# Moving one store, one turn of u and some sums between the slots of VectorE's program in a gated attention and MoE kernel

## The chip, the cores and the metric

The kernel runs on one core of a Trainium2 chip. The metric is the device time of one execution in microseconds (us); of several runs the median is taken. All times below are from such runs or from the hardware profile of one of them. Engines are named as in the profile: PE is TensorE, PEld its weight loads, DVE is VectorE, ACT is ScalarE, POOL is GpSimd, SP is SyncE, which here only issues DMAs.

## The reference

There are 8 batches of 3008 rows. For each batch the first half computes a gated attention without softmax, and the second half a feed-forward block on all 24064 rows:

```
scores = z @ z.T / S                 # z: 3008 x 64
attn   = maximum(scores, 0) ** 2
x      = u * (attn @ v)              # u, v: 3008 x 256
h      = x @ w_in                    # 256 -> 2048
g      = h * sigmoid(1.702 * h)
out    = g @ w_out                   # 2048 -> 256
```

## The kernel before

**Stages of a batch.** The rows of a batch are cut into six chunks of 512 columns (numbered 0 to 5; the last has 448). `attend` (L486) walks over a chunk in steps n = 0, 1, 2, ...; each step issues one or two matmuls on PE that add one key block's part to the chunk's accumulator (L529). A full chunk has 47 steps. Between the steps the main loop (L974) puts other work into each engine's queue: blocks of scores (`scores`, L247, squared by `square`, L268 and L282), loads, turns and sums. Since scores are symmetric, squared blocks are turned by DMA on SP (`turn_unit`, L310; L275, L289) and used for other chunks too. When a chunk is done, DVE multiplies its two accumulators with u (`gate`, L546), which gives x in the tile xt and frees the accumulators.

**Chunk 4** of batches 1 to 6 (`split`, L336) is done in another way, by `attend_split` (L426): seven products P1 to P7 instead of eight (Strassen's scheme), in 42 steps of two 256-column matmuls each (L440). The products need sums of score blocks, S1 to S4, and of value blocks, which DVE computes (`score_form`, L380, with lines L392, L394, L396, L383 for S1, S2, S4, S3; `value_forms`, L363). `fills` (L466) lists for each of these sums the slot (chunk, step) in which it goes into DVE's queue. The last of the three pairs of chunks (t = 2) has its eight half sums in chunk 4 itself. Some products share an accumulator: P6, P7 and P4 add to the bank of P1. So after the last step of P7, DVE must have added that bank to the tile ya (L458) before P4 may write to the bank again.

**Heads and tails.** The feed-forward part of a batch has 48 groups q = 0 to 47 (`up_group`, L569). A group is four matmuls to the tile hg (L584), a gelu on ACT to the tile gf (L597, with two buffers for hg and two for gf), and a scaled copy to the tile gt, by DVE (L603) or in some groups of the tail by ACT (L601). Groups 0 to 15 ("heads", LAGY = 16) are issued among the steps of chunk 4, from step 2 on; groups 16 to 47 come after chunk 5, one by one with the products of the output matrix (`pair_product`, L737, matmuls L757). These too are seven products instead of eight for each pair of chunks s = 0, 1, 2, and need block sums S1 to S4 of gt, 16 for each pair (`pair_sum`, L710: L719, L721, L723, L714). They wait in a list, SUMS. `some_sums(most)` (L621) puts the next one into DVE's queue, or the next two if more than `most` wait. In heads of a split batch it is called for q = 8, 9, 10, 12, 13 and 14 (L604), in the tail for each q (L598). A product whose sum is still missing takes it from the list itself (L754).

**Stores and turns.** `store` (L854) turns a chunk's result y into the tile yo on DVE (L859) and issues four or more DMAs on SP (L869). yo has one buffer, so the next store's turn waits until the DMAs of the one before have landed. Tile y has two buffers; the z of the next batch is staged in y buffers too (`stage_z`, L160, on POOL's queue in chunk 4, step 4). The results of the last two chunks of a batch are stored in the next batch: they wait in LAST2, and the main loop takes one at chunk 3, step 4, and one at chunk 3, step 26 (L987). `turn_u` (L210) turns a loaded chunk of u (tile uq, loaded on POOL's queue, L207) into the tile ut on DVE (L214), which `attend_split` first needs for P3 (L460). A small POOL copy, `hold` (L993), at chunk 4, step 4, keeps POOL's queue from loading u until the turned blocks of chunks 4 and 5 have landed.

**What sets the order.** Each engine works its queue in the order in which the program issues. Nothing reorders it. So a slot in these tables is a place in DVE's queue: an instruction that waits there holds all behind it.

```
slots += [(4, n) for n in (12, 12, 14, 14, 16, 18, 20, 22)]                      # L475
if not pair or LAGY > q >= (LAGY // 2 if split(b, NCH - 2) else 0) and q % 4 < 3:  # L604
    some_sums(8)
TURNS = {(1, NJ + 4): 2, (2, NJ + 4): 3, (4, 24): 4, (5, 8): 5}                  # L904
if (i, n) in ((3, 4), (3, 26) if more else (4, 14)) and LAST2:                   # L987
    LAST2.pop(0)()
```

Of the kernel before, what the change touches and what calls it, by code (L numbers as in the profile page):

```python
# [15 lines left out]
def kernel(  # L16
# [20 lines left out]
    NJ = (S + P - 1) // P  # L37
# [3 lines left out]
    NCH = (S + CH - 1) // CH  # L41
# [294 lines left out]
    def split(b, i):  # L336

        return i == NCH - 2 and 0 < b < B - 1
# [127 lines left out]
    def fills(b):  # L466

        VT.clear()
        SA.clear()
        at = {(0, 19): [lambda: pool.tensor_copy(VZ[TOP], V16[b][TOP, NJ - 1])]}  # L470
        slots = [(0, n) for n in (20, 23, 26, 28)] + [(1, n) for n in (27, 31, 35, 39, 43)]
        slots += [(2, n) for n in (19, 21, 23)]
        ops = [op for t in range(3) for op in value_forms(b, t)]
        slots += [(2, n) for n in (28, 33, 38, 43)] + [(3, n) for n in (30, 34, 41, 44)]
        slots += [(4, n) for n in (12, 12, 14, 14, 16, 18, 20, 22)]  # L475
        ops += [op for t in range(3) for op in score_forms(b, t)]
        assert len(ops) == len(slots)
        for where, op in zip(slots, ops):
            at.setdefault(where, []).append(op)
        return at  # L480
# [82 lines left out]
    def paired(b, s):  # L563

        return b < B - 1 or s < NCH // 2 - 1
# [3 lines left out]
    def up_group(b, q):  # L569
        s, r = divmod(q, 2 * NFG)  # L570
        pair = paired(b, s)
        if pair:
            fg, e = (TILES if q >= 2 * NFG or b else TILES0)[r // 2], r % 2
            if fg >= NFG // 2:
                e = 1 - e
            k = 2 * s + e
        else:
            k, fg = divmod(q, NFG)
        i, n = blocks(b)[k]
        hg = ps2.tile([P, FFG, CH], F32, name="hg", tag="ps2")  # L580
        for e in range(FFG):
            ff = fg * FFG + e
            for c in range(NCC):
                pe.matmul(  # L584
                    hg[:, e, :n], W1[:, c, ff * P:(ff + 1) * P], XT[b, i][:, c, :n],
                    start=(c == 0), stop=(c == NCC - 1),
                )
        if pair:
            if r % 2 == 0:
                GT[b, s, fg, "pair"] = pa.tile([P, FFG, 2, CH], F16, name="gt", tag="tt", bufs=14)  # L590
            g = GT[b, s, fg, "pair"][:, :, k % 2, :n]
        else:
            if fg % 2 == 0:
                GT[b, k, fg // 2] = pa.tile([P, CB, CH], F16, name="gt", tag="tt", bufs=14)
            g = GT[b, k, fg // 2][:, (fg % 2) * FFG:(fg % 2 + 1) * FFG, :n]
        gf = pw.tile([P, FFG, CH], F32, name="gf", tag="gf")
        act.activation(gf[:, :, :n], hg[:, :, :n], AF.Gelu_apprx_sigmoid, scale=1.0 / FSC)  # L597
        if pair and q >= LAGY:  # L598
            some_sums(3 if q % 2 else 8)
        if q >= LAGY and q % 8 in (1, 3, 5):  # L600
            act.activation(g, gf[:, :, :n], AF.Copy, scale=FSC)  # L601
        else:
            dve.tensor_scalar(g, gf[:, :, :n], FSC, None, ALU.mult)  # L603
        if not pair or LAGY > q >= (LAGY // 2 if split(b, NCH - 2) else 0) and q % 4 < 3:  # L604
            some_sums(8)
        if pair:
            some = (("S1", "S2", "S3"), ("S4",))[r % 2] if fg >= NFG // 2 else ()
            SUMS.extend([(s, "S1 S2 S4 S3".index(m), lambda m=m: pair_sum(b, s, fg - NFG // 2, m)) for m in some])
            SUMS.sort(key=lambda x: x[:2])
            if r == 2 * NFG - 2 and s == NCH // 2 - 1:  # L610
                some_sums(8)
        elif fg in (NFG - 3, NFG - 1):
            SUMS.extend([(s, 0, x) for x in left_sums(b, k, fg == NFG - 1)])
# [220 lines left out]
    LAST2 = []  # L834
# [39 lines left out]
    LAGY = 2 * NFG  # L874
# [26 lines left out]
    TURN0 = {(i, (38, 28)[i] if i < 2 else NJ + 4 if i < NCH - 1 else 12): i for i in range(NCH)}  # L901
    LOAD0 = {(1, 14): 2, (1, 40): 3, (4, 4): 4, (4, 36): 5}
    TURN = {(1, NJ + 4): 2, (2, NJ + 4): 3, (4, 10): 4, (5, 8): 5}
    TURNS = {(1, NJ + 4): 2, (2, NJ + 4): 3, (4, 24): 4, (5, 8): 5}  # L904
    LOADW = {
        (2, 16): 0, (3, 0): 2, (3, 9): 1, (3, 41): 3, (4, 28): 4, (4, 34): 5, (4, 40): 6, (5, 0): 7,
    }
# [51 lines left out]
    for b in range(B):  # L959
        nup = NCH * NFG  # L960
        more = b + 1 < B
        sched = SCHED0 if b == 0 else SCHED if more else SCHED_LAST
        turn, load = (TURN, LOAD) if b else (TURN0, LOAD0)
        if split(b, NCH - 2):
            turn, load = TURNS, LOADS
        head = 0
        for i in range(NCH):
            host = b + 1 if more and i == NCH - 1 else b
            if host > b:
                fill(host)  # L970
                LATE.append(host)
            if i == 0 and split(b, NCH - 2):
                extra = fills(b)
            for n, step in enumerate(attend_split(b, i) if split(b, i) else attend(b, i, b == 0 and i == 0)):  # L974
                if b == 0 and i == 0 and n in (5, 24):
                    load_u(0, n // 24)
                if b == 0 and i == 0 and n == 2:
                    copies = first_zt(3)
                if b == 0 and i == 0 and n == 3:
                    copies()  # L980
                if b == 0 and i == 0 and n in FIRST_CAST:
                    first_cast(FIRST_CAST[n], True)
                if b == 0 and i == 0 and n in FIRST_ZT:
                    first_zt(FIRST_ZT[n])()
                if (i, n) in turn:
                    turn_u(b, turn[i, n])
                if (i, n) in ((3, 4), (3, 26) if more else (4, 14)) and LAST2:  # L987
                    LAST2.pop(0)()
                if (i, n) == (0, 22) and COPY:
                    COPY.pop(0)()  # L990
                if split(b, i) and n == 4:
                    hold = pw.tile([P, 2], F16, name="hold", tag="hold")
                    pool.tensor_copy(hold, TT[b, i, NCH - 1][:, ::2, 0, 0])  # L993
                if (i, n) in load:
                    load_u(b, load[i, n])
                if b == 0 and (i, n) in CASTW:
                    cast_w(CASTW[i, n])
                if b == 0 and (i, n) in LOADW:
                    load_w(LOADW[i, n])
                if b == 0 and (i, n) == (NCH - 2, 6):  # L1000
                    stage_z(1, 0, tag="yo", bufs=1)
                if more and (i, n) == (NCH - 2, 4 if b else 16):
                    load_z(b + 1)
                if b == 0 and i == NCH - 1 and n in (8, 30, 42):
                    wsums.pop(0)()
                take(host, sched[i].get(n, 0))
                if split(b, NCH - 2):
                    for op in extra.get((i, n), ()):
                        op()
                if split(b, i):  # L1010
                    step()
                if i == full(b) and n >= HEAD and (n - HEAD) * LAGY // (2 * NJ - 10) >= head and head < LAGY:
                    up_group(b, head)
                    head += 1
                if not split(b, i):
                    step()
        late.sort(key=lambda t: t[0])
        if more:
            for i in range(2):
                load_u(b + 1, i)  # L1020
            for n0 in range(0, NJ, VB):
                load_v(b + 1, n0)
        prods = products(b)
        for q in range(head, nup):
            if more and q in (head + 14, head + 20):
                k = int(q == head + 20)
                turn_u(b + 1, k)
                load_u(b + 1, k + 2)
            up_group(b, q)
            if b == 0 and q == head + 3:  # L1030
                wsums.pop(0)()
            prods.pop(0)()
            for a_ in AFTER:
                a_[0] -= 1
            while AFTER and AFTER[0][0] < 0:
                AFTER.pop(0)[1]()
            if q >= 44 and late:
                late.pop(0)[1]()
        steps = prods
        for step in steps:  # L1040
            step()
            for sum_ in [SUMS.pop(0) for _ in range(min(len(SUMS), 1 + (len(SUMS) > 4)))]:
                sum_[2]()
            for _, turn_it in [late.pop(0) for _ in range(min(len(late), 1 + (len(steps) < 10)))]:
                turn_it()
        LATE.clear()
        if more:
            while late:
                late.pop(0)[1]()
            take(b + 1, 2)  # L1050
# [30 lines left out]
```

## Time and profile before

| | us |
|---|---|
| median of 3 runs | 1175.81 (1175.26 to 1176.27) |
| the profiled execution's own time | 1175.55 |
| its span, first to last instruction | 1173.7 |
| PE busy in the span | 1165.0 (99%) |
| DVE busy | 961.8 (82%) |
| ACT busy | 842.4 (72%) |
| POOL busy | 220.3 (19%) |

The own time is 1.9 us longer than the span, and 0.26 us under the median of the runs. In the rows of the profile a group of instructions has its line, engine, operation, written and read tiles, shape, count, busy time, mean duration, and the idle time of its engine just before it with what ended that. In rows of waits the three numbers are the total in us, the times and the longest. PE's matmuls are pipelined: a 512-column matmul lasts about 374 ns in the rows, but the next one starts 215 ns after it. So time that PE loses is read from the distances between starts, and idle time shows only a part of it.

### The profile page before, as it was taken

The page shows a single profiled execution, that of the slowest core. Times are in us where ns is not written, and L with a number is a line of the kernel's source. Part 1 is how long each engine was busy: PE and PEld are TensorE (multiplying, and loading weights), DVE is VectorE, ACT ScalarE, POOL GpSimd, SP SyncE. Part 2 cuts the span into 40 slices and gives each one's busy share as a digit, 9 for nine tenths or more (in the row PEclk, how much of TensorE's full clock was granted, in tenths as well). Part 3 has the DMA queues.
Part 4 walks back from the last instruction along what each step waited for, and adds up shares of the span by engine and source line. Part 5 has one row for each costly group of instructions (what it writes and reads, how often), then busy time and mean ns, then how long its engine had stood idle before and what let it go on. Part 6 is the DMA issues. An engine that isn't in the chain of part 4 may idle for free.

```text
span 1173.7 us, 21529 instructions
## 1 busy us (share of the span) xinstructions
PE 1165.0 (99%) x8212; PEld 593.6 (51%) x8212; DVE 961.8 (82%) x1596; ACT 842.4 (72%) x959; POOL 220.3 (19%) x307
## 2 busy tenths in 40 slices
PE   9999999999999999999999999999999999999998
PEld 3544455644455445554445545555444554544446
DVE  6779878988789886899868997789977899664876
ACT  7888864788647886478864787647867488672785
POOL 3033200432004320042101421024210251001000
PEclk9999999999999999999999999999999999999999
DMA  9997399854997559885498755996559975698023
GB/s 223 200 158 106 80 172 158 99 93 93 168 155 100 90 108 171 148 108 87 96 172 153 105 88 109 169 150 95 91 102 174 146 104 85 117 166 141 1 36 73
DMA packets 459033, 143.54 MB, mean 122 GB/s; under 512 B 424624, under 2 KB 453040, under 8 KB 458928
## 3 DMA queue, kind: packets, MB, share of 16 engines
q1 hardware_dynamic: 402464, 102.36, 52.6%
q0 software_dynamic: 55104, 38.49, 21.5%
q8 instruction: 64, 1.05, 0.4%
q10 hardware_dynamic: 1360, 1.31, 0.4%
q14 instruction: 41, 0.34, 0.1%
HBM read 60.29 MB, written 24.64 MB: 72 GB/s over the span
## 4 chain that ended last, share of the span: by engine, by line
PE 90%; DVE 6%; ACT 2%; issue 1%; DMA 1%; SPq 0%; DVEq 0%; ACTq 0%
PE o L529 33%; PE hg L584 24%; PE st L757 23%; PE sc L247 6%; PE oz L440 2%; DVE gt L603 2%; PE st L805 1%; ACT gf L597 1%; DVE s L719 1%; PE yp L731 1%; DVE ut L214 1%; DMA tt<-a 1%; ACT rl L268 0%; DVE s L721 0%; DVE sa L396 0%
## 5 line engine op out<-in xcount | busy, mean ns | idle before, releaser
L597 ACT ACTIVATE gf<-hg 128x1024 f32<-128x1024 f32 (+1 forms) x384 | 383.2, 1003 | 121.9 <-PE hg L584 95.4
L268 ACT ACTIVATE rl<-sc 128x1024 f16<-128x1024 f32 (+1 forms) x301 | 288.9, 992 | 152.9 <-PE sc L247 107.7
L584 PE MATMUL hg<-xt,W 128*128 128x512 f16 (+1 forms) x1408 | 353.4, 374 | 1.2 <-ACT gf L597 0.8
L529 PEld LDWEIGHTS <-V 64*128 64x128 f16 (+1 forms) x3810 | 208.9, 94 | 197.6 <-POOLq L88 5.5
L529 PE MATMUL o<-a,V 64*128 64x512 f16 (+3 forms) x2254 | 291.2, 368 | 0.1
L603 DVE TENSOR_SCALAR gt<-gf 128x1024 f16<-128x1024 f32 (+1 forms) x288 | 204.8, 713 | 65.2 <-ACT gf L597 63.5
L282 DVE TENSOR_TENSOR a<-rl 128x1024 f16<-128x1024 f16 (+1 forms) x266 | 175.2, 672 | 76.2 <-ACT rl L268 75.1
L584 PEld LDWEIGHTS <-W 128*128 128x128 f16 x1536 | 149.5, 98 | 158.0 <-issue 4.8
L207 POOL DMA_DIRECT2D uq<-in_u_dram x168 | 117.3, 708 | 344.7 <-DVE ut L214 158.6
L529 PE MATMUL o<-tt,V 64*128 64x512 f16 (+1 forms) x1278 | 166.9, 376 | 0.0
L247 PE MATMUL sc<-ZT 64*128 64x512 f16 (+3 forms) x688 | 118.1, 357 | 0.6 <-ACT ZT L145 0.3
L757 PEld LDWEIGHTS <-WT 128*128 128x128 f16 x736 | 72.0, 98 | 79.5 <-issue 0.6
L601 ACT ACTIVATE gt<-gf 128x1024 f16<-128x1024 f32 (+1 forms) x96 | 98.1, 1022 | 3.1
L757 PE MATMUL st<-gt,W 128*128 128x512 f16 (+1 forms) x368 | 89.9, 370 | 0.0
L757 PE MATMUL st<-s,WT 128*128 128x512 f16 (+1 forms) x368 | 89.1, 370 | 0.0
L757 PE MATMUL st<-gt,WT 128*128 128x512 f16 (+1 forms) x368 | 88.7, 370 | 0.0
L993 POOL COPY hold<-tt 128x2 f16<-128x2 f16 x6 | 2.3, 391 | 434.0 <-DMA tt<-a 434.0
L757 PEld LDWEIGHTS <-W 128*128 128x128 f16 x552 | 53.8, 98 | 58.2
L859 DVE STREAM_TRANSPOSE yo<-y 128x1024 f32<-128x1024 f32 (+1 forms) x46 | 56.1, 1220 | 15.7 <-DMA out_dram<-yo 15.0
L247 PEld LDWEIGHTS <-ZT 64*128 64x128 f16 x688 | 39.8, 94 | 44.6 <-issue 9.3
L774 DVE SCALAR_TENSOR_TENSOR y<-st,y 128x512 f32<-128x512 f32 (+1 forms) x69 | 45.7, 663 | 19.4 <-PE st L757 18.5
L719 DVE TENSOR_TENSOR s<-gt 128x1024 f16<-128x1024 f16 (+1 forms) x92 | 60.6, 659 | 1.1
(101 smaller groups left out, 1002.8 us busy)
## 6 DMA issues: line engine op xcount, KB each, us to landing
out_dram<-yo SPq DMA_DIRECT2D x156, 128.0 KB, 2.8
uq<-in_u_dram POOLq DMA_DIRECT2D x140, 128.0 KB, 3.5
V<-in_v_dram POOLq DMA_DIRECT2D x35, 256.0 KB, 6.2
tt<-a SPq DMA_TRANSPOSE x232, 3.4
uq<-in_u_dram POOLq DMA_DIRECT2D x28, 112.0 KB, 5.8
out_dram<-yo SPq DMA_DIRECT2D x28, 96.0 KB, 3.3
uq<-in_u_dram SPq DMA_DIRECT2D x20, 128.0 KB, 4.2
wst<-in_moe_w_in_dram POOLq DMA_DIRECT2D x4, 512.0 KB, 6.0
```

Of the source, the lines that this page charges most:

```text
L207: eng.dma_start(uq[k * QW:(k + 1) * QW, :n // QW].rearrange("t q c k -> t q (c k)"), src[:, :, cs])
L247: pe.matmul(sc[:, r, :q1 - q0], zt[h, 2 * kp + r, :], zt[h].rearrange("d n p -> d (n p)")[:, q0:q1], start=True, stop=True,)
L268: act.activation(rl[:, :, :n], sc[:, :, :n], AF.Relu, scale=csc)
L282: dve.tensor_tensor(a[:, :, :n], rl[:, :, :n], rl[:, :, :n], ALU.mult)
L529: ins = pe.matmul(acc[c][:, :n], channels(V16[b][h, j], c), weights(b, i, j)[h], start=(k, m) == first[c], stop=(k, m) == final[c],)
L584: pe.matmul(hg[:, e, :n], W1[:, c, ff * P:(ff + 1) * P], XT[b, i][:, c, :n], start=(c == 0), stop=(c == NCC - 1),)
L597: act.activation(gf[:, :, :n], hg[:, :, :n], AF.Gelu_apprx_sigmoid, scale=1.0 / FSC)
L601: act.activation(g, gf[:, :, :n], AF.Copy, scale=FSC)
L603: dve.tensor_scalar(g, gf[:, :, :n], FSC, None, ALU.mult)
L719: dve.tensor_tensor(s_, a21, a22, ALU.add)
L757: pe.matmul(bank, right[:, ff], lhs[:, f], start=new and ff == 0, stop=ff == NFF // 2 - 1, skip_group_check=True,)
L859: dve.transpose(yo[:, :m].rearrange("p q c k -> p q k c"), Y[b, k][:, :, :n].rearrange("p k (q t) -> p q k t", t=QW),)
```

## The change

Four edits, which act on batches 1 to 6 (the second store: in batches 1 to 6 too, since batch 0 has none to take and batch 7 keeps its slot).

1. The second left-over store is taken at chunk 4, step 1, and no longer at chunk 3, step 26.
2. The eight half sums S1, S2, S4, S3 of the last pair (t = 2) go into DVE's queue at steps 8, 9, 11, 12, 14, 15, 17, 18 of chunk 4, and no longer at 12, 12, 14, 14, 16, 18, 20, 22.
3. u of chunk 4 is turned at step 20 and no longer at step 24.
4. In the heads of a split batch `some_sums` is called for q = 8, 9, 12, 13 and no longer for q = 10 and 14.

```diff
-        slots += [(4, n) for n in (12, 12, 14, 14, 16, 18, 20, 22)]
+        slots += [(4, n) for n in (8, 9, 11, 12, 14, 15, 17, 18)]
...
-        if not pair or LAGY > q >= (LAGY // 2 if split(b, NCH - 2) else 0) and q % 4 < 3:
+        if not pair or LAGY > q >= (LAGY // 2 if split(b, NCH - 2) else 0) and q % 4 < (2 if split(b, NCH - 2) else 3):
             some_sums(8)
...
-    TURNS = {(1, NJ + 4): 2, (2, NJ + 4): 3, (4, 24): 4, (5, 8): 5}
+    TURNS = {(1, NJ + 4): 2, (2, NJ + 4): 3, (4, 20): 4, (5, 8): 5}
...
-                if (i, n) in ((3, 4), (3, 26) if more else (4, 14)) and LAST2:
+                if (i, n) in ((3, 4), (4, 1) if more else (4, 14)) and LAST2:
                     LAST2.pop(0)()
```

## Prediction

> **What bounds the kernel now.** I read the busy times first, then the chain, then what PE waits for, and last the rows in order of time around chunk 4 of the batches 1 to 6, where all four edits act.
>
> ```profile
> PE 1165.0 (99%) x8212; PEld 593.6 (51%) x8212; DVE 961.8 (82%) x1596; ACT 842.4 (72%) x959; POOL 220.3 (19%) x307
> ...
> PE 90%; DVE 6%; ACT 2%; issue 1%; DMA 1%; SPq 0%; DVEq 0%; ACTq 0%
> ```
>
> PE sets the end. How much it still loses is not in the 99%, so I measured the distances between the starts of its matmuls: a full 512-column one is followed after 215 ns, a half-array pair after about 215 ns too, a 256-column one after 109 ns. With such paces all 8212 matmuls need 1150.2 us. From first to last start they take 17.6 us more. Some 6 us of these lie in the first 40 us, which no edit touches, and about 7 us in pieces of some 0.1 us where one kind of matmul follows another. What waits for another engine in the later batches is little, and all of it is in or just behind chunk 4:
>
> ```profile
> PE oz L440 <- DVE ya L458: 1.0, 6, 0.2
> PE hg L584 <- ACT gf L597: 0.8, 2, 0.6
> ```
>
> These are idle times, and they are too small, since a row's end is the modelled end of a pipelined matmul. In distances it looks so (PE in batch 2, whose chunk 4 begins at 350.79):
>
> ```profile
> 370.72 0.27 PE L440 MATMUL oz<-tt,VZ 128*128 128x256 f16 x1
> 371.15 0.38 PE L440 MATMUL oz<-tt,vt 128*128 128x256 f16 x2 [0.16 <-DVE ya L458]
> ```
>
> The second, the first matmul of P4, starts 0.43 us after the one before it; 0.11 is the pace, so 0.32 is lost. The same place costs 0.32 to 0.33 in each of the six batches: 1.95 us. Matmuls of hg that waited for gf lose 0.24 (batch 1, at 223.7), 0.24 (batch 4, 657.7), 0.77 and 0.38 (batch 5, 788.2 and 801.3), 0.27 and 0.24 (batch 6, 934.7 and 947.3): 2.13 us. One wait for rl in chunk 5 of batch 2 (379.7) loses 0.26. **Sum 4.34 us.** That is the most that the change can bring back.
>
> Who is late there? DVE's rows:
>
> ```profile
> 347.64 0.22 DVE L285 TENSOR_TENSOR a<-rl 128x128 f16<-128x128 f16 x1
> 350.15 1.25 DVE L859 STREAM_TRANSPOSE yo<-y 128x1024 f32<-128x1024 f32 x1 [2.29 <-DMA out_dram<-yo]
> 351.32 0.65 DVE L392 TENSOR_TENSOR sa<-tt 128x1024 f16<-128x1024 f16 x1
> ...
> 354.08 1.28 DVE L546 TENSOR_TENSOR xt<-o,ut 128x512 f16<-128x512 f32 x2
> 355.28 1.43 DVE L603 TENSOR_SCALAR gt<-gf 128x1024 f16<-128x1024 f32 x2
> ```
>
> The second store stands 2.29 us still until the first store's DMAs have landed (six times, 15.0 us in all by DVE's waits). Everything behind it is late: xt, whose accumulators PE left at 350.8, comes at 354.08, and the first gt at 355.28, though its gelu ended at 353.55. Later in the same head:
>
> ```profile
> 366.22 0.41 DVE L383 TENSOR_TENSOR ad<-ad 128x512 f16<-128x512 f16 x1
> 366.55 1.23 DVE L214 STREAM_TRANSPOSE ut<-uq 128x1024 f32<-128x1024 f32 x1
> ...
> 369.49 0.68 DVE L721 TENSOR_TENSOR s<-s,gt 128x1024 f16<-128x1024 f16 x1
> 370.09 0.68 DVE L603 TENSOR_SCALAR gt<-gf 128x1024 f16<-128x1024 f32 x1
> 370.69 0.41 DVE L458 TENSOR_TENSOR ya<-ya,oz 128x256 f32<-128x256 f32 x1
> ```
>
> From 364.67 DVE has no idle time. The add of P7, ready when PE ends P7's last step at about 368.2 (step 31 starts at 367.97), is done at 371.1.
>
> **The change part by part.** Times in chunk 4 are now counted from its first matmul (+0 is 350.79). Occupancy is the distance of starts in a busy stretch: gt and a 128x1024 sum 0.60, a 128x512 half sum 0.33, a turn of u or y 1.17, the 256-column add 0.33. The order of each engine's instructions before and after shows that PE, ACT, POOL and SP keep theirs; only DVE's changes. No DMA is moved past another on SP or POOL.
>
> *Store later.* Removed from chunk 3: 2.29 us idle and 1.17 us of work. The four score sums and al then follow 347.9 at once. al must wait for ACT's rl of L263, which ends at 349.5; then 0.27, 0.60 and 0.60 bring DVE to about 351.0, and xt goes at +0.2 instead of +3.3 and ends at +1.4. The store follows, +1.4 to +2.6; its buffer has landed by then (-0.7, in batch 5 +0.2). The first gelu ends at +2.76, so gt of group 0 waits for its gelu, not for DVE. The price if that cover is gone: 1.17 us ahead of gt. Today gt of group 0 is 1.7 us behind its gelu in batch 2, and PE loses nothing there; so 1.17 fits. SP's DMAs of this store start at +2.4 now, held by al's two transposes; the turn's end at +2.6 delays them by 0.3. Behind them on SP stand the transposes of the next batch's z, which wait for their z until +11. On POOL, the z load into the store's y buffer issues at +5.4, after four loads of u; y is free at +2.6. Gain: the two early losses of hg, 0.77 and 0.27, go, since gt is no longer late.
>
> *Half sums and u sooner.* No work is added. The first half sum (step 8, +4.35 on PE) stands behind gt of group 2, ready at +5.6, and the turned blocks which it reads land at +1.3 to +2.7. u lands at +7.8 to +10.6 in the six batches, step 20 is at +11.3 on PE. DVE reaches u's turn at +13.2 by the count below. So neither adds a wait. Nothing waits for u's turn today (P3's xt comes 6 us after it), so there is nothing to gain by that alone; if u landed later by the whole spread of the six batches (2.8 us), DVE would stand 0.2 us, with all that is behind it. Bounds 0 and 0.2 us a batch; I take 0.
>
> *Two sums fewer.* The heads now hold five block sums, not seven: 1.2 us less DVE work, 0.6 of it ahead of the add of P7.
>
> Run through by hand with these occupancies and the gelus at PE's pace: gt of group 7 at +12.6, u to +14.4, gt of groups 8 to 10 with two sums to +17.4. Then DVE waits for the gelu of group 11, which ends at +18.2, gt to +18.8, and the add of P7 from +18.8 to +19.2. P4 would start at +20.04 without a stall. So the add has 0.8 us in hand, where it was 0.3 late. gt of group 9 ends at +16.2, ahead of the gelu of group 11 (+17.16) which needs its buffer; so the later losses of hg (0.24, 0.24, 0.38, 0.24) go too, and the last gt is some 1.4 us sooner, which covers the 0.26 in chunk 5.
>
> POOL's two copies of z (L174) lie at +11.0 and +13.2. Beside the first one gt took 1.12 us and not 0.68. In the new order a gt and the turn of u lie there. With 0.44 for each the add of P7 still comes after the same gelu of group 11, so nothing is charged. The Trainium skill (SBUF — State Buffer, section Who interferes with whom) says that VectorE and GpSimd share one pair of ports, held for a whole instruction, which speaks against packing this head denser; by it a VectorE instruction could stand for up to a whole copy, 0.82 to 1.11 us in the rows, and two of those would eat the 0.8 in hand and leave the 1.95. The row of 1.12 shows such a stretch, the half sum at 364.05 beside the second copy, 0.41 as always, shows none.
>
> *The tail.* The two sums return there, 1.2 us of DVE a batch. By the order, one comes in groups 25 to 26, where DVE stood idle 1.06 us before 404.45, the other ahead of gt of group 31 (414.09); until DVE is idle again, at 421.3 and 424.1 (0.07 and 1.13), gts there are 0.6 late. PE's cover: the gelu of group 33 ends at 415.8, the next user of its hg buffer starts at 417.17; 1.36 in hand, 0.75 after. The sums that products of s = 0 and 1 take have 2.4 us or more in hand. So 0.
>
> The Trainium skill (Perfetto Trace Analysis, section Identifying the Most-Contended Engine) says to optimise the engine that is most contended first, and to judge TensorE by LDWEIGHTS busy, not matmul busy. PEld's 51% would mean much room on PE, and an edit that only shuffles DVE would bring nothing. The starts every 215 ns speak for a full PE; by the rule the sum is 0, by the rows 4.3.
>
> **The sum.** 4.34 at most; I keep 0.2 for leftovers in batch 5 and 6, whose first store lands latest, and take 4.1. Against the profiled execution: 1175.55 - 4.1 = 1171.45. Its median stands 0.26 higher: 1175.81 - 4.1 = **1171.7**.
>
> **The rivals.**
> - *Half of it.* P7's add stays late, or the wait for DMAs does not go but passes to the next instruction: the order shows that the sums behind the old place of the store now have DMA waits which the store's had covered. If these end only with the first store's landing, DVE reaches xt at about +2 and the store still lies before gt. Then either the 1.95 or the 2.1 stays: about 1173.4 to 1173.9, say 1173.5. For it: DVE is 95% busy in the head (22.9 of 24 us). Against it: these sums read turned blocks that landed before.
> - *Nothing.* The 4 us come back as waits elsewhere, for u at step 20 or z: 1175.8. Against it: POOL and SP keep order and start times within 0.3 us.
> - *Slower.* The tail becomes DVE's: two sums a batch with all their 1.2 us in front of gts, 7.2 us in six batches less 4.3, so 1178.7. It decides once gts of groups 30 to 36 are more than 1.36 us later than now. For it: DVE has no idle time from 408 to 421. Against it: by the order only 0.6 comes there.
>
> **How the numbers follow.** Forecast 0.60, half 0.24, nothing 0.07, slower 0.09. About 0.2% (2.35 us, to 1173.46) is what a measurement can tell here. Half of the second case lies under that: faster 0.72, same 0.19, slower 0.09. The range reaches from all 4.34 gone with half a us of run-to-run spread, 1170.9, over the second case to 1175.0, and leaves out most of the last two.
>
> **What would show it.** In the new profile DVE's wait of yo for its own DMAs (15.0) is near 0, xt of chunk 3 comes within 0.3 us of PE's end, PE's rows of waits no longer have ya L458 nor gf L597, and PE's way from first to last start is 1163.7 us, not 1167.8; PE's busy time falls little. Wrong it would be if P4 still started late, if u's turn waited for uq, or if hg waited in groups 30 to 36.

## The result and the profile after

The changed kernel takes **1170.42 us** (median of 6 runs, 1170.10 to 1171.06); the kernel before took 1175.92 in the 6 runs beside it (1175.26 to 1176.56). The ratio is 0.9954 (95% interval 0.9941 to 0.9967): 5.5 us or 0.46% less. A second comparison on another occasion gave 1171.13 against 1175.74, ratio 0.9964 (0.9951 to 0.9976). The change is faster, by more than forecast: 1170.42 lies 0.5 us under the range.

The page of the changed kernel, busy times and chain:

```profile
span 1168.5 us, 21541 instructions
...
PE 1161.9 (99%) x8212; PEld 589.5 (50%) x8212; DVE 958.7 (82%) x1596; ACT 842.1 (72%) x959; POOL 224.3 (19%) x307
...
PE 99%; ACT 1%; issue 0%; DVE 0%
```

The chain is now almost PE's alone; DVE's 6% in it are gone. PE's busy time fell by 3.1 us of the span's 5.2: part of a wait was booked as busy, as in the kernel before, where P4 started 0.32 us late and its row showed 0.16 us of that as idle.

What PE waits for, all rows of that view:

```profile
PE w L101 <- DVE nil L76: 1.2, 1, 1.2
PE o L529 <- DVE a L282: 0.4, 1, 0.4
PE sc L247 <- ACT ZT L145: 0.3, 1, 0.3
PE sc L247 <- ACT rl L268: 0.2, 1, 0.2
```

All four lie in the first 30 us. Neither ya L458 nor gf L597 is left. DVE around the start of chunk 4 of batch 2, which now begins at 349.80:

```profile
346.65 0.22 DVE L285 TENSOR_TENSOR a<-rl 128x128 f16<-128x128 f16 x1
346.79 0.68 DVE L392 TENSOR_TENSOR sa<-tt 128x1024 f16<-128x1024 f16 x1
347.51 0.69 DVE L394 TENSOR_TENSOR sa<-sa,tt 128x1024 f16<-128x1024 f16 x1
348.54 0.36 DVE L264 TENSOR_TENSOR al<-rl 128x384 f16<-128x384 f16 x1 [0.34 <-ACT rl L263]
...
350.02 1.28 DVE L546 TENSOR_TENSOR xt<-o,ut 128x512 f16<-128x512 f32 x2
351.22 1.28 DVE L859 STREAM_TRANSPOSE yo<-y 128x1024 f32<-128x1024 f32 x1
352.59 0.80 DVE L603 TENSOR_SCALAR gt<-gf 128x1024 f16<-128x1024 f32 x1
```

The 2.29 us of standing still are gone, xt comes at +0.22, the store at +1.42, the first gt at +2.79, when its gelu ends. Later in the head, DVE and then PE:

```profile
366.75 0.86 DVE L603 TENSOR_SCALAR gt<-gf 128x1024 f16<-128x1024 f32 x1
367.98 0.69 DVE L603 TENSOR_SCALAR gt<-gf 128x1024 f16<-128x1024 f32 x1 [0.37 <-ACT gf L597]
368.59 0.42 DVE L458 TENSOR_TENSOR ya<-ya,oz 128x256 f32<-128x256 f32 x1
```

```profile
369.65 0.27 PE L440 MATMUL oz<-tt,VZ 128*128 128x256 f16 x1
369.76 0.38 PE L440 MATMUL oz<-tt,vt 128*128 128x256 f16 x2
```

DVE has time to wait for gf; P7's add is done at 369.01, 0.75 us before P4, which starts 0.11 us after the matmul before it: no loss.

PE issues the same 8212 matmuls in the same order in both kernels, so each one's start can be subtracted from that of its twin. That tells where the time came from; the table sums it over the six batches for every run below (one profiled execution each, in us gained against the one before; "early" is from chunk 4's first matmul to group 7, "later" from there to P4, "P4" the start of P4, "chunk 5" from P4's end to group 16, "tail" the groups 16 to 47). Batch 7 is in no column. The opening (first 45 us) differs from execution to execution whatever the kernel.

| run | what it has | median gain | ratio, 95% interval | opening | early | later | P4 | chunk 5 | tail |
|---|---|---|---|---|---|---|---|---|---|
| changed kernel | all four edits | 5.50 | 0.9954 (0.9941 to 0.9967) | 0.33 | 1.06 | 1.14 | 1.95 | 0.88 | 0.00 |
| e11_changed | the same again | 4.61 | 0.9964 (0.9951 to 0.9976) | 0.55 | 1.06 | 1.14 | 1.95 | 0.90 | 0.00 |
| e1_store | store | 0.72 | 0.9995 (0.9984 to 1.0006) | 0.36 | 1.06 | -0.47 | 0.02 | 0.01 | 0.00 |
| e2_half | half sums | 2.82 | 0.9967 (0.9954 to 0.9979) | 0.52 | 0.29 | 0.75 | 1.29 | 0.33 | 0.00 |
| e3_turn | u | 2.65 | 0.9965 (0.9949 to 0.9981) | 0.20 | 0.15 | 0.90 | 1.60 | 0.56 | 0.00 |
| e4_block | block sums | 1.98 | 0.9981 (0.9972 to 0.9991) | 0.30 | 0.26 | -0.33 | 1.95 | 0.12 | 0.00 |
| e5_no_store | all but the store | 4.42 | 0.9960 (0.9948 to 0.9973) | 0.11 | 0.30 | 1.14 | 1.95 | 0.90 | 0.00 |
| e6_no_block | all but block sums | 5.29 | 0.9954 (0.9941 to 0.9968) | -0.06 | 1.07 | 1.14 | 1.72 | 0.67 | 0.00 |
| e7_store_block | store, block sums | 3.05 | 0.9971 (0.9959 to 0.9982) | 0.26 | 1.07 | -0.38 | 1.95 | 0.14 | 0.00 |
| e10_half_turn | half sums, u | 3.92 | 0.9971 (0.9959 to 0.9983) | 0.42 | -0.05 | 1.14 | 1.69 | 0.76 | 0.00 |
| e8_none | all, and no block sums in heads | 4.55 | 0.9958 (0.9946 to 0.9970) | 0.04 | 1.06 | 1.14 | 1.95 | 0.90 | -0.75 |
| e9_first | first store sooner, nothing else | 4.24 | 0.9966 (0.9953 to 0.9978) | -0.38 | 1.06 | 1.14 | 1.37 | 0.02 | 0.00 |
| e12_no_copy | POOL's copy of z replaced | 3.30 | 0.9967 (0.9955 to 0.9979) | 0.41 | -0.28 | 1.14 | 1.23 | -0.01 | 0.00 |
| e13_store_no_copy | store, POOL's copy replaced | 4.72 | 0.9968 (0.9950 to 0.9986) | 0.20 | 1.06 | 1.14 | 1.46 | 0.00 | 0.00 |

The intervals are 2 to 4 us wide, so they don't tell neighbouring rows apart (that of e1_store holds 1); the columns from the traces do. They come from one execution each, but the two of the changed kernel agree within 0.02 in all five columns behind the opening.

### The profile page after: what moved, and what is told of

It reads as the page before. It is cut to its first block, busy times and chain, and to the rows that moved or that the text cites. A ratio compares the mean times of both kernels' runs of the same rounds, so it can differ in the third digit from the quotient of the medians.

```text
span 1168.5 us, 21541 instructions
## 1 busy us (share of the span) xinstructions
PE 1161.9 (99%) x8212; PEld 589.5 (50%) x8212; DVE 958.7 (82%) x1596; ACT 842.1 (72%) x959; POOL 224.3 (19%) x307
## 3 DMA queue, kind: packets, MB, share of 16 engines
q10 hardware_dynamic: 1360, 1.31, 0.4%
## 4 chain that ended last, share of the span: by engine, by line
PE 99%; ACT 1%; issue 0%; DVE 0%
PE o L529 36%; PE hg L584 28%; PE st L757 23%; PE sc L247 6%; PE oz L440 5%; PE st L805 1%; PE yp L731 1%; ACT rl L268 0%; PE w L101 0%; ACT ZT L145 0%; PE zp L137 0%; DVE y L823 0%; ACT zst L128 0%; DVE nil L76 0%
## 5 line engine op out<-in xcount | busy, mean ns | idle before, releaser
L597 ACT ACTIVATE gf<-hg 128x1024 f32<-128x1024 f32 (+1 forms) x384 | 383.8, 1003 | 116.3 <-PE hg L584 100.5
L529 PEld LDWEIGHTS <-V 64*128 64x128 f16 (+1 forms) x3810 | 205.9, 94 | 202.7 <-POOLq L88 6.6
L207 POOL DMA_DIRECT2D uq<-in_u_dram x168 | 120.7, 728 | 341.1 <-DVE ut L214 157.6
L774 DVE SCALAR_TENSOR_TENSOR y<-st,y 128x512 f32<-128x512 f32 (+1 forms) x69 | 45.8, 663 | 19.7 <-PE st L757 18.8
L721 DVE TENSOR_TENSOR s<-s,gt 128x1024 f16<-128x1024 f16 (+1 forms) x92 | 60.5, 657 | 0.8
L723 DVE TENSOR_TENSOR s<-gt,s 128x1024 f16<-128x1024 f16 (+1 forms) x92 | 59.4, 662 | 2.0 <-DVE s L721 0.9
```

What stands on the lines that cost most here:

```text
L207: eng.dma_start(uq[k * QW:(k + 1) * QW, :n // QW].rearrange("t q c k -> t q (c k)"), src[:, :, cs])
L529: ins = pe.matmul(acc[c][:, :n], channels(V16[b][h, j], c), weights(b, i, j)[h], start=(k, m) == first[c], stop=(k, m) == final[c],)
L721: dve.tensor_tensor(s_, ST[b, s, "S1", m], a11, ALU.subtract)
```

## The experiments

**The theories.** Queue theory: the losses have separate causes along DVE's queue. The standing still of the store makes only the first gts late; P7's add is late because DVE has no idle time from group 8 on; each edit shortens a part of that. Store theory: the 15 us of standing still are behind everything. Theory of shares: each edit brings a share of its own. All kernels below differ from the kernel before only by the diffs named.

**Each edit alone.** The diffs are the four of the change, one each.

> Only the second store is moved (chunk 4, step 1). Queue theory: the lost time has separate causes; the 2.3 us for which the store stands still only make the first gts late, and DVE has caught up by the gt of group 8 (it waits there for gf, 0.21 us). So only the two early losses of hg in batches 5 and 6 go (0.77 + 0.27 = 1.04): about 1174.9, with the late add of P7 (0.32 in each batch) still there. Store theory: the store's standing still (15.0 us in all) makes the whole head late, so it alone brings nearly all of the gain: about 1171, add of P7 in time.

Measured 1174.72 against 1175.44. The early column has its 1.06, P4's waits stand as they were, the later losses grew by 0.47. The store theory falls. Yet DVE reached P7's add even later, at +20.18 in batch 2 and not +19.90; POOL's and DVE's rows of that run show why:

```profile
361.87 1.18 POOL L174 COPY zst<-zst 128x768 f16<-128x768 f16 x1 [2.83 <-DMA zst<-in_z_dram]
364.24 0.82 POOL L174 COPY zst<-zst 128x768 f16<-128x768 f16 x1 [1.19 <-DMA zst<-in_z_dram]
```

```profile
363.85 0.41 DVE L383 TENSOR_TENSOR a<-a 128x512 f16<-128x512 f16 x1
364.28 1.33 DVE L603 TENSOR_SCALAR gt<-gf 128x1024 f16<-128x1024 f32 x1
365.53 0.68 DVE L719 TENSOR_TENSOR s<-gt 128x1024 f16<-128x1024 f16 x1
...
370.61 0.41 DVE L458 TENSOR_TENSOR ya<-ya,oz 128x256 f32<-128x256 f32 x1
```

The gt beside the second copy lasts 1.33 us and not 0.68, and it is the last one before the stretch without idle time. I come back to that.

> Only the eight half sums are sooner. Queue theory: one half sum (0.33) leaves the stretch without idle time ahead of P7's add, which is 0.27 to 0.3 late, so 1.6 to 1.95 us of P4's waits go; the early losses of hg stay or grow by some tenths: about 1174.3. Store theory: nothing goes, about 1175.9.

Measured 1172.62, better than expected by 1.7. P4 got 1.29, but the later waits for gf 0.75 and chunk 5 0.33 as well, which I had not counted for this edit. In the kernel before DVE stood idle for 0.40, 0.20 and 0.22 us ahead of the gts of groups 2, 3 and 6; half sums that come sooner find room there. P4's part of the gain comes nearly whole or not at all: its 0.32 goes in four batches and stays in batches 2 and 5. In batch 2 POOL's second copy met the block sum behind the gt of group 8:

```profile
363.81 1.18 POOL L174 COPY zst<-zst 128x768 f16<-128x768 f16 x1 [1.42 <-DMA zst<-in_z_dram]
```

```profile
364.22 1.31 DVE L719 TENSOR_TENSOR s<-gt 128x1024 f16<-128x1024 f16 x1
```

That sum takes 0.68 elsewhere; the add starts at +20.06. In batch 3 the copy lies 0.8 us sooner in the chunk and meets no such sum, and the add starts at +19.30.

> Only u of chunk 4 is turned 4 steps sooner. Queue theory: the turn takes the place of DVE's idle 0.21 us ahead of group 8's gt, so the add of P7 is 0.2 to 0.6 sooner and gt of group 9 too: 1.2 to 3.5 us go, about 1173.5; early losses of hg stay. Store theory: nothing goes, about 1175.9.

Measured 1172.79, in the expected range: P4 1.60 (its 0.32 in five of the six batches), later 0.90, chunk 5 0.56. With e2_half and this one the store theory, which gave them nothing, falls a second time.

> Only two block sums fewer in the heads. Queue theory: 0.6 us of DVE less ahead of P7's add, 1.2 less ahead of the last gt: P4's six waits (1.95), the waits of chunk 5's second score block for the buffer of the last hg (six times 0.09) and the one wait for rl (0.25) go, losses of hg (2.1) stay: 2.7 us, about 1173.1. Store theory: at most some tenths, about 1175.7.

Measured 1173.46. P4's 1.95 went whole, as expected. But the later losses grew by 0.33 and chunk 5 gained 0.12 where 0.8 was expected. PE's waits between 160 and 1000 us have one row:

```profile
PE hg L584 <- ACT gf L597: 0.8, 2, 0.4
```

One of the two is the wait of hg ahead of P4 in batch 2 (369.48), the other the early loss of batch 5 (787.77); the sums taken out lie behind the gts that these wait for. In batch 2, where the later losses grew, the gt of group 8 lasts 1.21 us beside POOL's second copy (364.19).

**Combinations.** The diffs are again those of the change, the named ones left out. The four alone add up to 8.2, together they bring 5.5 or 4.6: they overlap.

> Half sums, u and block sums as in the changed kernel, the second store at its old place. Queue theory: only the early losses of hg in batches 5 and 6 come back (up to 1 us, perhaps some tenths more since half sums now stand in front of late gts): about 1171.4. Theory that each edit carries its own share, as the four alone add up (0.7 + 2.8 + 2.7 + 2.0 = 8.2 against 5.5 together): also about 1171; store theory: 1175.

1171.66 against 1176.08, as expected. Only the early column lacks (0.30, not 1.06). The theory of shares had said about the same, so this run speaks against the store theory alone.

> Store, half sums and u as in the changed kernel, block sums as before (six calls in the heads). Queue theory: P7's add needs only 0.3 us, and half sums and u already give it more, so nothing or some tenths (chunk 5's waits for the last hg buffer, six times 0.09) come back: 1170.4 to 1171.0. Theory of shares: the 2.0 that block sums brought alone are missing, 1172.4.

1170.79, a gain of 5.29. All columns are there without that edit but 0.23 of P4 and 0.21 of chunk 5: the theory of shares (1172.4) falls. With the other three in, the block sums' edit brings these 0.44 us, and not its 1.98 alone.

> Store and block sums alone, half sums and u as before. Queue theory: P7's add is in time and the early losses are gone; later losses of hg around groups 12 and 13 (1.1, in the run with block sums alone up to 0.4 in a batch) stay: 1172.4 to 1173. Theory of shares: 0.7 + 2.0, 1173.1.

1173.03, at the upper end. Here both theories said nearly the same; the column of the later losses (-0.38) is the queue theory's.

> Half sums and u sooner, store and block sums as before. Queue theory: the two overlap; P7's add, chunk 5 and the later losses of hg are all served, only the early ones of batches 5 and 6 stay: 4.0 to 4.6 gained, about 1171.6. Theory of shares: 2.8 + 2.7 = 5.5, 1170.4.

1171.82, a gain of 3.92: just under the queue theory's 4.0 to 4.6 and far from the 5.5 of shares; half sums and u serve the same losses.

> The changed kernel once more. The losses listed before and the six of 0.09 in chunk 5 make 4.9; so about 5 us under the kernel before on this chip, and within 0.5 of the kernel without the block sums' edit. If the 5.5 us of the first comparison are all of the change: 5.5.

1171.13 against 1175.74, 4.6 less. With the first comparison the gain is 4.6 to 5.5; the trace's columns give 5.0 in both executions, without the opening. In batch 7 both lose 0.2 to 0.3 again at one matmul, which leaves 4.7 to 4.8.

**How much the tail can take.** This is the rival of the slower tail.

```diff
-... and q % 4 < (2 if split(b, NCH - 2) else 3):
+... and q % 4 < (0 if split(b, NCH - 2) else 3):
```

> The changed kernel with no block sums at all in the heads of split batches: five more go to the tail, 3 us of DVE more a batch there. Queue theory: the head has no loss left, so nothing is gained there; in groups 16 to 24 DVE then has two sums and a gt a group, 1.8 us against PE's 1.73, and products take their sums nearly as they come: between 1170.4 and 1173. The rival of the slower tail: hg waits for gf in the tail, 6 batches with 1 us or more each, 1176 or above.

1171.53. The tail column has -0.75 for 3 us more of DVE work in each of six tails, 18 us in all. One such place, PE and ACT in batch 2:

```profile
419.81 1.03 PE L757 MATMUL st<-s,W 128*128 128x512 f16 x4
420.83 0.48 PE L584 MATMUL hg<-xt,W 128*128 128x384 f16 x2
```

```profile
412.67 1.02 ACT L597 ACTIVATE gf<-hg 128x1024 f32<-128x1024 f32 x1 [1.30 <-DVE gt L603]
...
418.80 1.06 ACT L601 ACTIVATE gt<-gf 128x1024 f16<-128x1024 f32 x1
419.77 1.01 ACT L597 ACTIVATE gf<-hg 128x1024 f32<-128x1024 f32 x1
```

Four matmuls at 0.215 from 419.81 end their issue at 420.67; hg starts at 420.83, once the gelu that holds its buffer ends at 420.78. ACT is late there since the gelu at 412.67, which waited 1.30 us for DVE's gt; in the changed kernel the same gelu (411.79) waits for PE instead. So the mechanism of the rival exists. It takes more than the changed kernel's 1.2 us a batch to start it; there the column is 0.00.

**Standing still or place, and POOL's copies.** The store was left where it was, and the store before it taken sooner, so that its DMAs land in time:

```diff
-                if (i, n) in ((3, 4), (3, 26) if more else (4, 14)) and LAST2:
+                if (i, n) in ((2, 30) if more else (3, 4), (3, 26) if more else (4, 14)) and LAST2:
```

> The kernel before, with the first left-over store taken at chunk 2, step 30 (batches 1 to 6), the second at its old place: the second no longer stands still, and no other edit is in. Queue theory: as with the store moved alone, only the early losses of hg go, 0.7 to 1.0: about 1174.9. If the store's place, and not its waiting, made gts late: nothing, 1175.8.

1171.50 against 1175.74: over four times what I expected. That refutes the queue theory in the form in which I had it. Batch 2 in that run, POOL and DVE:

```profile
359.04 1.37 POOL L174 COPY zst<-zst 128x768 f16<-128x768 f16 x1 [1.49 <-DMA zst<-in_z_dram]
361.64 1.01 POOL L174 COPY zst<-zst 128x768 f16<-128x768 f16 x1 [1.22 <-DMA zst<-in_z_dram]
```

```profile
361.89 1.31 DVE L603 TENSOR_SCALAR gt<-gf 128x1024 f16<-128x1024 f32 x1
...
364.46 0.69 DVE L603 TENSOR_SCALAR gt<-gf 128x1024 f16<-128x1024 f32 x1
...
370.14 0.41 DVE L458 TENSOR_TENSOR ya<-ya,oz 128x256 f32<-128x256 f32 x1
```

The first store's four DMAs start on SP at 341.34 and not at 344.69, so SP comes sooner to the last turned blocks of chunks 4 and 5 (345.90 and 348.62, not 347.19 and 350.49). The blocks land sooner, POOL's wait ahead of hold ends at -0.06 and not at +2.00 (chunk 4 begins at 350.62), z follows, and its two copies lie at +8.4 and +11.0 where they lay at +11.0 and +13.2. A gt is still lengthened, to 1.31, but before group 8 (364.46), where DVE has caught up again. The add of P7 starts at +19.52. P4 could start at +20.04 with an add of 0.41: so the margin is there, and 1.37 of P4's 1.95 goes.

The next two tell whether POOL's copies did it. z is loaded twice by DMA, and POOL copies nothing:

```diff
-        pool.dma_start(zst[:, :full, 0, :], src)
...
+        for c in range(2):
+            pool.dma_start(zst[:, :full, c, :], src)
...
-            pool.tensor_copy(zst[:, :, 1, :], zst[:, :, 0, :])
```

> The kernel before, with the z of the next batch loaded twice by DMA in place of POOL's copy of it (L174); no edit of the change. Theory that POOL's copies lengthen DVE's instructions beside them (0.41 to 1.04, 0.68 to 1.3): the two stretches ahead of P7's add in each head are gone, so the add starts at +19.5 or sooner and P4 no longer waits: 2 us or more gained, about 1173.5. Theory that only DVE's own queue counts: nothing, 1175.7; more z DMAs on POOL's queue could also cost, at most some tenths in chunk 5.

1172.55 against 1175.85. No edit of the change is in, the second store stands still as ever, and 3.3 us go, though the early losses grew by 0.28. DVE in batch 2 (chunk 4 begins at 350.02):

```profile
357.27 0.92 DVE L603 TENSOR_SCALAR gt<-gf 128x1024 f16<-128x1024 f32 x1 [0.20 <-ACT gf L597]
...
361.30 0.70 DVE L603 TENSOR_SCALAR gt<-gf 128x1024 f16<-128x1024 f32 x1 [0.24 <-ACT gf L597]
...
363.90 0.69 DVE L603 TENSOR_SCALAR gt<-gf 128x1024 f16<-128x1024 f32 x1 [0.27 <-ACT gf L597]
...
369.58 0.41 DVE L458 TENSOR_TENSOR ya<-ya,oz 128x256 f32<-128x256 f32 x1
```

The two gts that took 1.12 and 1.03 before (362.07 and 364.67 there) take 0.70 and 0.69. The one at 357.27 takes 0.92, as it took 0.94 before: POOL issues z's DMAs beside it. The add starts at +19.56, the later losses are gone whole and P4's in greater part.

> As before it, with the second store at chunk 4, step 1. Theory of POOL's copies: the store moved alone brought only 0.7 since the second copy lay beside the last gt ahead of P7 (1.33 us in batch 2); without copies both early losses and P4's waits go, 4 us or more, about 1171.5. Theory that the store's place in the head takes what its waiting gives: as with the store alone plus nothing, about 1174.9.

1171.13, 4.7 us gained, 0.4 more than expected. This kernel and e1_store differ only in POOL's copies and the z loads in their place, and the columns of the two are 3.0 us apart (later 1.6, P4 1.4): the store moved alone brought 0.7 since POOL's copies held DVE up, not since the store's own 1.17 us in the head cost it. The gt of group 8 starts at +13.84 in all six batches of e13_store_no_copy; in the kernel before it starts at +14.17 to +14.65 in five of them, and in batch 2 at +13.88 with 0.34 of lengthening in itself. So the causes of P7's late add are DVE's full queue from group 8 on **and** POOL's copies, in that stretch or ahead of it. Only 0.3 us are wanting, so less of either gives back most or all of P4's 1.95: 1.29, 1.60 and 1.95 for the three edits of the queue, 1.23 and 1.46 without copies.

## Why the prediction was wrong

- **The list of losses was right but short.** Early 1.04 forecast, 1.06 measured; later 1.10 and 1.14; P4 1.95 and 1.95. In chunk 5 I had one wait of 0.26 and the trace gave back 0.88. The step of the prediction that failed is the term for chunk 5 in its sum, and behind it the sentence "about 7 us in pieces of some 0.1 us where one kind of matmul follows another": six of those pieces were no such thing. In the kernel before, batch 2, PE and ACT:

```profile
374.89 0.92 PE L529 MATMUL o<-a,V 64*128 64x448 f16 x8
375.74 0.28 PE L247 MATMUL sc<-ZT 64*128 64x256 f16 x2
```

```profile
374.66 1.02 ACT L597 ACTIVATE gf<-hg 128x1024 f32<-128x1024 f32 x1 [1.21 <-DVE gt L603]
```

  The score block starts at 375.74, 0.09 late, right after the gelu of group 15 ends (375.68): it waits for the last hg's buffer (sc and hg take turns in the same two, L239 and L580), and that gelu waits for DVE. In the changed kernel the same pair starts without it:

```profile
373.50 0.92 PE L529 MATMUL o<-a,V 64*128 64x448 f16 x8
374.25 0.27 PE L247 MATMUL sc<-ZT 64*128 64x256 f16 x2
```

  Six times 0.09 is 0.55. So "4.34 is the most" should have been 4.89.
- **The leftover was not there.** I kept 0.2 for batches 5 and 6; both early losses went whole (0.76 and 0.27). So of the 0.9 us between 4.1 and the columns' 5.0, chunk 5 has 0.6 and this term 0.2.
- **The rest is open.** 0.33 us of the difference between the two profiled executions lies in the opening, where no edit acts (the fourteen executions above differ there by 0.9). Against it 0.2 us is lost in batch 7, where no edit acts either: a weight load waits 0.53 us for the DMA of a turned block (1070.50) that waited 0.25 us before. The second execution of the changed kernel loses 0.3 at the same matmul, and none of the other kernels does, so this may be the change's doing; its cause was not followed. The runs' medians put the gain at 5.5 once and 4.6 once, on both sides of the traces' 4.7 to 4.8. A range whose low end stood on a sum that was 0.55 short missed the first by 0.5 us; that the second lies within it is the spread between occasions and no merit of the sum.
- **The order of events was right.** xt at +0.2 (measured +0.22), the store from +1.4 (+1.42), the add of P7 from +18.8 (+18.79), nothing lost to u or z, nothing in the tail. Distances from first to last start: 1163.7 forecast, 1162.7 measured. That PE's busy time would fall little was wrong: 3.1 us went.
- **POOL's copies were priced too low as a cause.** "Nothing is charged" holds for the new order: in batch 2 the first copy lengthens a half sum (1.04), the second lies beside the turn of u, which keeps its 1.23. But in the order before the copies made some of the 0.3 by which P7's add was late; e12_no_copy shows it. The prediction read the half sum beside the second copy, 0.41, as no lengthening, and missed the next row, a gt of 1.03 and not 0.68 which begins under the same copy:

```profile
364.03 1.11 POOL L174 COPY zst<-zst 128x768 f16<-128x768 f16 x1 [1.39 <-DMA zst<-in_z_dram]
364.05 0.41 DVE L383 TENSOR_TENSOR a<-a 128x512 f16<-128x512 f16 x1
...
364.67 1.03 DVE L603 TENSOR_SCALAR gt<-gf 128x1024 f16<-128x1024 f32 x1 [0.21 <-ACT gf L597]
```

  The section of the Trainium skill weighed there (SBUF — State Buffer, Who interferes with whom) was the better guide to the cause. That it is the ports that collide, no run here shows; and the most that a copy added in the rows shown is 0.65 (1.33 against 0.68), less than a whole copy.
- **The rivals.** "Half" and "slower" did not happen. Half's mechanism, a wait for the first store's landing that passes to the next instruction, is small: in the changed kernel's rows al waits 0.34 for ACT; in e7_store_block it waits three times for those DMAs, 1.0 us in all, with the early column whole. The slower tail starts beyond 1.2 us a batch: 3 us more lost 0.75 in all (e8_none). The Trainium skill's rule (Perfetto Trace Analysis, Identifying the Most-Contended Engine), judged by weight loads alone as the prediction did, would have given no gain; PE's own distances gave it. The page names MFU, the share of peak FLOPs, beside the weight loads, and the prediction left that half out.

None of the runs beats the changed kernel by more than the runs vary. In both of its executions with a trace no wait of PE for DVE or gf is left between 160 and 1000 us.

## What to carry to other kernels

When one engine is nearly full, list its losses by the distances between starts, and look for the releaser of each piece, also of those of 0.1 us: a piece that repeats once a batch at the same instruction is a wait until it is shown not to be. Where an instruction is late by 0.3 us at the end of a stretch without idle time, anything that shortens the stretch by 0.3 can cure it, so the gains of such edits overlap and must not be added. Before moving work in a queue, look what the other engines do beside it: the same instruction cost 0.68 or 1.33 us by its place.

## What the runs showed of the hardware

A POOL copy of 128x768 f16 and some DVE instructions last longer side by side than alone. In the changed kernel's batch 2 (POOL's first copy at 361.40, 1.01 us) the half sum that starts 0.25 us after it lasts 1.04 us and not 0.42:

```profile
361.40 1.01 POOL L174 COPY zst<-zst 128x768 f16<-128x768 f16 x1 [2.89 <-DMA zst<-in_z_dram]
...
361.65 1.04 DVE L383 TENSOR_TENSOR ad<-ad 128x512 f16<-128x512 f16 x1
...
363.22 1.23 DVE L214 STREAM_TRANSPOSE ut<-uq 128x1024 f32<-128x1024 f32 x1
363.48 0.82 POOL L174 COPY zst<-zst 128x768 f16<-128x768 f16 x1 [1.07 <-DMA zst<-in_z_dram]
```

A gt (f32 to f16 in SBUF) goes from 0.68 to 1.31 or 1.33 in the same way, and POOL's copy from 0.82 to as much as 1.37. The turn of u beside the second copy is not lengthened, nor that copy. A gt can take longer beside POOL's DMA issues too, 0.92 in e12_no_copy, where POOL copies no z. Which of POOL's and DVE's accesses collide was not tried further.
